# Attention, dense layer and routed experts on one core: value products of two head pairs in one group, transposed weights in the score tile, a later fetch for the first expert

## The chip, the cores and the metric

The kernel runs on one core of a Trainium2 chip. The core has TensorE (PE, with its weight loads as PEld), VectorE (DVE), ScalarE (ACT), GpSimd (POOL), and SyncE (SP), whose queue issues most DMAs here; each works through its instructions in order, and they meet by semaphores. The metric is the device time of one execution in microseconds (us); less is better.

## What is computed

Three steps, each feeding the next, all in fp32 with B, H, S, D = 4, 8, 576, 64:

```python
scores = q @ k.T / 8                         # per batch and head: 576 x 576
kth = 32nd largest of each row               # keep the 32 largest
attn = softmax(where(scores >= kth, scores, -1e9))
x = attn @ v                                 # -> 2304 tokens x 512
h = x @ w_in                                 # 512 x 2048
g = where(h >= 1, h, where(h <= -1, 0, (h + 1)**2 / 4))
x = g @ w_out                                # 2048 x 512
logits = x @ w_gate                          # 8 experts, 288 tokens each,
                                             # filled greedily by largest logit
out[mask_e] = relu(x[mask_e] @ w1[e]) @ w2[e]
```

## The kernel before

The work is recorded as a list of operations with their costs and data dependencies (`Program`), and a planner (`issue`, line 166) gives each engine its order: a list schedule by a rank that the code sets (`P.rank`), refined over ten rounds with the planner's own costs. Operations under `P.group()` stay together on TensorE. There are two such programs, one for each phase; a wait on the chip follows from the data, whatever the planner thought.

First phase (line 365): a loop over 4 batches, 5 blocks of query rows (four of 128, one of 64, j = 4) and 4 pairs of heads. For each pair, `scores` (494) makes two score tiles of 128x576 in a tile of the ring `t_s` (three tiles of two heads each) by way of PSUM bank `pS`; `topk` (541) finds the 32 largest on VectorE, and ScalarE and GpSimd turn the scores into unscaled weights in place. Then `values` (624): TensorE transposes the weights in pieces of 128x128 to `pPT`, ScalarE copies them to `pt`; the last 64 columns of both heads and the reciprocal sums go through `pQ` to `tr`. The products with the values run head by head: c = 0 to 3 are 128 rows deep with 64 columns of values `v` (a 128x64 shape), c = 4 is 64 rows deep (`u`, a 64x64 shape), in two groups. fp32 products take two passes each, so a full pair has 16 passes of the first kind and 4 of the second. VectorE scales the result to `xf`, and ScalarE and GpSimd split it into a high and a low part in `XB` (the dense layer's products are three products of such parts).

The dense layer (`ffn_block`, 687) takes 256 tokens at a time as soon as they are there; its products are planned among the attention's. Block 8, the last, leaves its second product to the second phase. The weights of the dense layer come as 64-bit words and are decoded at the start (`weights`, 444), beside the first pairs.

Second phase (831): `route` (1082) finds one expert's 288 tokens, `places` (1167) their places and indices, `gathers` (1205) fetch the tokens from DRAM with three indirect DMAs from GpSimd, and `expert` (1218) fetches that expert's two matrices with eight DMAs of 512 KB on SP's queue into four buffers `raw`, splits them into high and low parts, and multiplies. For the first expert the gathered tokens meet those of the last dense block in PSUM (`gathered`, 889). The steps of eight experts are planned together.

Of the kernel before, what the change touches and what calls it, by code (L numbers as in the profile page):

```python
# [9 lines left out]
F32 = mybir.dt.float32  # L10
# [37 lines left out]
NF, NM, NSM, NXF, NTR, NQR = 5, 2, 3, 1, 1, 2  # L48
# [230 lines left out]
def kernel(ctx: ExitStack, tc: tile.TileContext, qm, qt, kT, vm, vt,  # L279
# [85 lines left out]
    def first_phase(exact, actx):  # L365
# [78 lines left out]
        def weights(exact):  # L444
            raws = [stage[:, 1024 * i:1024 * i + 1024] for i in range(2)]
            raws += [t.rearrange("p a x -> p (a x)")[:, :1024] for t in (t_s(), t_s(), t_s())[1:]]
            t32s = [stage[:, 2048:2560], spare] + [t_pt().rearrange("p c x -> p (c x)") for _ in range(2)]
# [26 lines left out]
        def load_pair(b, p):  # L474
# [13 lines left out]
            Y.dma_start(out=u_t[:, 0, :], in_=vt[b, :, p])  # L488
            Y.dma_start(out=u_t[:64, 1, :], in_=vt[b, 64:, p])
# [134 lines left out]
        def values(b, j, p, r, s_sb, rinv, wide):  # L624
            P.rank = r + R_PV
            _, v_t, u_t = KV[b, p]
            tail, rb, acc = pQ[:, 0:128], pQ[:, 128:256], pQ[:, 256:384]
            full = j < 4
            w = 128 if full else 64
            pts = []  # L630
            for i in range(2 if full else 1):
                o_ = 64 * i
                with P.group():
                    for c in range(4):
                        T.transpose(pPT[:, 128 * c:128 * c + 128], s_sb[:, i, o_ + 128 * c:o_ + 128 * c + 128], ident)
                pt = t_pt()
                A.activation(pt.rearrange("p c x -> p (c x)"), pPT, AF.Copy)
                pts.append(pt)
            flat = s_sb.rearrange("p a x -> p (a x)")
            tr = t_tr()  # L640
            if full:
                A.activation(wide.rearrange("p (a x) -> p a x", a=2), rinv[:, :2].unsqueeze(2).to_broadcast([128, 2, 64]),
                             AF.Copy)
            with P.group():
                if full:
                    T.transpose(tail, flat[:, 512:640], ident)
                    T.transpose(rb, wide, ident)
                else:
                    T.transpose(tail[:64, :], flat[:, 512:576], ident)
                    T.transpose(rb, rinv[:, 0:1].to_broadcast([128, 128]), ident)  # L650
            if full:
                A.activation(tr.rearrange("p a x -> p (a x)"), pQ[:, :256], AF.Copy)
            else:
                A.activation(tr[:64, 0, :], tail[:64, :], AF.Copy)
                A.activation(tr[:, 1, :], rb, AF.Copy)
            for cs in ((0, 1), (2, 3, 4)):
                with P.group():
                    for c in cs:
                        for h in range(2):
                            hs = slice(64 * h, 64 * h + 64)  # L660
                            if c < 4:
                                rhs = pts[h][:, c, :] if full else pts[0][:, c, hs]
                                T.matmul(acc[hs, :w], v_t[:, c, hs], rhs, start=(c == 0), stop=False)
                            elif full:
                                T.matmul(acc[hs, :w], u_t[hs, 0, :], tr[hs, 0, :], start=False, stop=True)
                            else:
                                T.matmul(acc[hs, :w], u_t[:64, h, :], tr[:64, 0, hs], start=False, stop=True)
            xf = t_xf()
            if full:
                V.tensor_tensor(out=xf, in0=acc, in1=tr[:, 1, :], op=ALU.mult)  # L670
            else:
                for h in range(2):
                    hs = slice(64 * h, 64 * h + 64)
                    V.tensor_tensor(out=xf[hs, :64], in0=acc[hs, :64], in1=tr[hs, 1, hs], op=ALU.mult)
            t0 = b * S + 128 * j
            c0 = 0
            while c0 < w:
                k, off = divmod(t0 + c0, BLK)
                n = min(w - c0, BLK - off)
                if k not in xT:  # L680
                    xT[k] = t_x()
                xh, xl = xT[k][:, 0, p, off:off + n], xT[k][:, 1, p, off:off + n]
                A.activation(xh, xf[:, c0:c0 + n], AF.Copy)
                G.tensor_tensor(out=xl, in0=xf[:, c0:c0 + n], in1=xh, op=ALU.subtract)
                c0 += n
# [80 lines left out]
        def routing_constants():  # L766
            raw = t_pt().rearrange("p c x -> p (c x)")
# [14 lines left out]

        if not exact:
# [21 lines left out]
        t_pt.reset()  # L805
        at, blk = 0.0, 0
# [24 lines left out]
    def second_phase(exact, rctx):  # L831
# [250 lines left out]
        def route(ph):  # L1082
# [331 lines left out]
```

## Time and profile before

| | us |
|---|---|
| median of 3 runs | 1151.74 |
| lowest and highest | 1150.81, 1154.38 |
| the profiled execution's own time | 1145.99 |
| its span, first to last instruction | 1143.7 |
| TensorE busy, share of the span | 1062.0, 93% |
| VectorE busy | 931.2, 81% |
| ScalarE busy | 805.0, 70% |
| GpSimd busy | 697.5, 61% |
| mean granted TensorE clock | 0.963 |

Shares over the whole span mix stages: decoding and the first attention pairs (0 to 120 us), attention and dense layer together (120 to 795), the rest of the dense layer (to 836), routing and the first expert (to 883), and the experts (to the end). TensorE's instructions are pipelined and their ends are modelled, so its busy time includes overlap; differences of starts tell what a group really takes.

### The profile page before, as it was taken

What the parts mean: (1) busy time and instruction counts of PE and PEld (TensorE: products, weight loads), DVE (VectorE), ACT (ScalarE), POOL (GpSimd) and SP (SyncE); (2) the same over time, 40 slices, a digit from 0 to 9 for tenths busy, and PEclk for the clock granted to TensorE, in tenths of its full rate; (3) what the DMA queues carried; (4) which work ended last, traced back from release to release, by engine and by line L of the source; (5) the groups of instructions that cost most, each with busy time, mean ns of one, the idle gap of its engine ahead of it and who ended that gap; (6) DMA issues with size and microseconds to landing.
All of it is one profiled execution on the core that took longest, in us unless ns stands there. A gap on an engine that the chain in (4) does not pass through costs nothing. (4 is left out here: it accounts for less than half of the span.)

```text
span 1143.7 us, 24385 instructions
## 1 busy us (share of the span) xinstructions
PE 1062.0 (93%) x8359; PEld 940.0 (82%) x8359; DVE 931.2 (81%) x2923; ACT 805.0 (70%) x1835; POOL 697.5 (61%) x872
## 2 busy tenths in 40 slices
PE   3677799999999999999999999999997999999995
PEld 2456588888888888898888888888976899999995
DVE  7899999889999999989899999984257997776430
ACT  8899987778888888877888988874313455445541
POOL 6988988977876988757688777763211152223111
PEclk9976599999999999999999999999988999999998
DMA  9744332352212352322134312212315664556500
GB/s 268 220 156 157 111 117 70 109 165 66 92 54 61 96 175 66 92 73 80 61 101 129 93 52 70 82 59 64 117 53 184 208 200 160 169 189 204 175 22 24
DMA packets 62197, 132.81 MB, mean 116 GB/s; under 512 B 15984, under 2 KB 24432, under 8 KB 62064
## 3 DMA queue, kind: packets, MB, share of 16 engines
q1 hardware_dynamic: 58992, 121.73, 33.8%
q0 software_dynamic: 3072, 9.44, 2.5%
q8 instruction: 67, 1.10, 0.4%
q14 instruction: 66, 0.54, 0.2%
HBM read 116.98 MB, written 14.16 MB: 115 GB/s over the span
## 5 line engine op out<-in xcount | busy, mean ns | idle before, releaser
L267 PE MATMUL pH<-XB,W 128*128 128x256 f32 (+1 forms) x2496 | 360.0, 291 | 0.7 <-DVE spare L267 0.3
L267 PEld LDWEIGHTS pH<-XB,W 128*128 128x128 f32 x2496 | 326.5, 189 | 9.7 <-issue 2.9
L267 DVE MAX8 m<-f 128x8 f32<-128x288 f32 x720 | 302.6, 449 | 2.2
L267 POOL TENSOR_TENSOR s<-s,f 128x576 f32<-128x576 f32 x144 | 204.3, 1430 | 30.0 <-ACT f L267 29.1
L267 DVE MATCH_REPLACE8 f<-m,f 128x288 f32<-128x288 f32 x432 | 190.7, 444 | 0.5 <-issue 0.3
L267 PE MATMUL pX<-W,XB 128*128 128x512 f32 x608 | 184.7, 411 | 0.7 <-ACT XB L267 0.7
L267 PE MATMUL pS<-XB 128*128 128x288 f32 (+2 forms) x672 | 145.2, 327 | 31.9 <-POOL XB L267 15.3
L267 POOL TENSOR_TENSOR XB<-stage,XB 128x512 fp32r<-128x512 f32 (+1 forms) x96 | 126.9, 1323 | 59.1 <-ACT XB L267 35.1
L267 PEld LDWEIGHTS pS<-XB 128*128 128x128 f32 x672 | 107.9, 203 | 52.4 <-DVE f L267 18.5
L267 ACT ACTIVATE s<-s,sm 128x576 f32<-128x576 f32 x144 | 111.3, 773 | 22.4 <-POOL s L267 21.3
L267 PEld LDWEIGHTS pX<-W,XB 128*128 128x128 f32 x608 | 107.7, 191 | 19.4 <-issue 2.9
L1210 POOL DMA_INDIRECT xg<-dram_x,idx x24 | 35.4, 1476 | 123.6 <-issue 49.4
L267 ACT ACTIVATE f<-s,t_all 128x576 f32<-128x576 f32 x144 | 108.2, 772 | 2.5
L267 ACT ACTIVATE s<-pS 128x576 f32<-128x576 f32 x144 | 92.7, 643 | 23.2 <-PE pS L267 22.8
L267 PE MATMUL pX<-XB,W 128*128 128x288 f32 x768 | 108.6, 297 | 0.0
L267 DVE TENSOR_TENSOR f<-pS,s 128x288 f32<-128x288 f32 x198 | 86.4, 450 | 22.5 <-ACT s L267 9.2
L267 DVE TENSOR_TENSOR W<-raw,W 128x1024 fp32r<-128x1024 f32 x64 | 76.8, 1218 | 33.5 <-ACT W L267 33.3
L267 PEld LDWEIGHTS pX<-XB,W 128*128 128x128 f32 x768 | 103.5, 188 | 0.0
L267 PE MATMUL pPT<-ident,s 128*128 128x128 f32 x576 | 92.8, 286 | 8.3 <-ACT s L267 6.8
L267 ACT ACTIVATE pt<-pPT 128x512 f32<-128x512 f32 x144 | 84.9, 589 | 17.5 <-PE pPT L267 17.1
L267 PE MATMUL pQ<-pt,v 128*64 128x128 f32 (+1 forms) x1280 | 91.7, 283 | 5.4 <-ACT tr L267 5.2
L1304 POOL DMA_INDIRECT out_dram<-yo,idx x24 | 26.9, 1120 | 109.8 <-ACT yo L267 106.3
(209 smaller groups left out, 1910.2 us busy)
## 6 DMA issues: line engine op xcount, KB each, us to landing
wl<-dram_wlo SPq DMA_DIRECT2D x64, 512.0 KB, 3.4
raw<-in_w_dram SPq DMA_DIRECT2D x64, 512.0 KB, 4.8
qr<-in_qm_dram SPq DMA_DIRECT2D x128, 64.0 KB, 2.4
stage<-in_w_in_dram SPq DMA_DIRECT2D x14, 512.0 KB, 4.2
stage<-in_w_out_dram SPq DMA_DIRECT2D x14, 512.0 KB, 3.3
stage<-in_kT_dram SPq DMA_DIRECT2D x48, 144.0 KB, 2.8
dram_wlo<-wl SPq DMA_DIRECT2D x8, 512.0 KB, 3.1
v<-in_vm_dram SPq DMA_DIRECT2D x16, 256.0 KB, 3.2
```

Source lines behind the costliest of these rows:

```text
L267: P.add(eng, lambda: fn(*args, **kw), cost, reads, writes, lat)
L1210: return nc.gpsimd.indirect_dma_start(out=xg[:, g, :], out_offset=None, in_=x2d[:, :], in_offset=bass.IndirectOffsetOnAxis(ap=idx[:, g:g + ...
L1304: st = nc.gpsimd.indirect_dma_start(out=out, out_offset=bass.IndirectOffsetOnAxis(ap=idx[:, g:g + 1], axis=0), in_=yo, in_offset=None)
```

## The change

- `values` is cut in two. `transposed` makes the transposes of one pair and writes them back over the pair's score tile (its columns 0 to 511, 640 to 1151 and, for the last columns, 512 to 639), so the tiles `pt` and the wide `tr` go; `tr` now holds only the reciprocal sums. Their room goes to a fourth score tile, `s_last`, which also takes the decoded words that `pt` held at the start.
- `values` then runs once for two pairs: 20 products of each pair in one group, to two places of `pQ`, then for both the scaling (into the score tile's first 128 columns, so `xf` goes too) and the split.
- The tail product runs on all 128 rows: each head's 64 rows of `u` stand in their own half, the other half is set to zero once, at the start, and `u` is loaded by two DMAs of 64 rows. For j = 4 the last 64 columns are transposed twice so that they stand in both halves.
- The loads of the next batch's keys and values are recorded after the second pair of a group.
- In `places` the index is written by the reduction itself; `pos` is bounded before instead of the index after.
- For expert 0 the four fetches of the second matrix now wait until the three gathers have landed (they name `xg` as read).

```diff
@@ first_phase @@
+        us = [t_u() for _ in range(4)]
-        t_s = ring(3, tiles=s_tiles)
+        s_last = apool.tile([128, 2, S], F32, name="s3")
+        t_s = ring(4, tiles=s_tiles + [s_last])
-        t_pt = ring(2, [128, 4, 128], F32, "pt")
-        t_tr = ring(NTR, [128, 2, 128], F32, "tr")
-        t_xf = ring(NXF, [128, 128], F32, "xf")
+        t_tr = ring(NTR, [128, 128], F32, "tr")
@@ load_pair @@
-            Y.dma_start(out=u_t[:, 0, :], in_=vt[b, :, p])
-            Y.dma_start(out=u_t[:64, 1, :], in_=vt[b, 64:, p])
+            for h in range(2):
+                Y.dma_start(out=u_t[64 * h:64 * h + 64, h, :], in_=vt[b, 64 * h:64 * h + 64, p])
@@ values @@
+        def transposed(b, j, p, r, s_sb, rinv, wide):
...
+            def last():
+                with P.group():
+                    if full:
+                        T.transpose(tail, flat[:, 512:640], ident)
+                        T.transpose(rb, wide, ident)
+                    else:
+                        T.transpose(tail, flat[:, 448:576], ident)
+                        T.transpose(tail[:64, :], flat[:, 512:576], ident)
+                        T.transpose(rb, rinv[:, 0:1].to_broadcast([128, 128]), ident)
+                A.activation(flat[:, 512:640], tail, AF.Copy)
+                A.activation(tr, rb, AF.Copy)
+            if not full:
+                last()
+            pts = []
+            for i in range(2 if full else 1):
+                pt = flat[:, 640 * i:640 * i + 512]
+                with P.group():
+                    for c in range(4):
+                        T.transpose(pPT[:, 128 * c:128 * c + 128], pt[:, 128 * c:128 * c + 128], ident)
+                A.activation(pt, pPT, AF.Copy)
...
+        def values(b, j, ps, r, made):
...
+            accs = [pQ[:, 256 + 128 * n:384 + 128 * n] for n in range(2)]
             with P.group():
...
-                                T.matmul(acc[hs, :w], u_t[:64, h, :], tr[:64, 0, hs], start=False, stop=True)
+                                T.matmul(acc[hs, :w], u_t[:, h, :], flat[:, 512:640] if full else flat[:, 512:640][:, hs],
+                                         start=False, stop=True)
...
+                xf = flat[:, :128]
...
+        P.rank = -10.0
+        for u_t in us:
+            G.memset(u_t[64:, 0, :], 0.0)
+            G.memset(u_t[:64, 1, :], 0.0)
...
-                    values(b, j, p, at, s_sb, rinv, wide)
+                    made.append(transposed(b, j, p, at, s_sb, rinv, wide))
+                    if p % 2:
+                        values(b, j, (p - 1, p), at, made)
+                        made = []
                     at += 1.0 if j < 4 else 0.6
-                    if j == 4 and b + 1 < B:
-                        P.rank = at + R_K
-                        load_pair(b + 1, p)
+                    if j == 4 and b + 1 < B and p % 2:
+                        for x in (p - 1, p):
+                            P.rank = at + R_K
+                            load_pair(b + 1, x)
@@ route, places @@
+            most = rt([128, NT], F32, "most")
+            V.tensor_scalar(most, tk, 2.0 * N * E, None, op0=ALU.mult)
...
-            V.scalar_tensor_tensor(out=pos, in0=sc, scalar=pS[:, 1, 8:9], in1=tk, op0=ALU.add, op1=ALU.mult)
+            V.scalar_tensor_tensor(out=pos, in0=sc, scalar=pS[:, 1, 8:9], in1=most, op0=ALU.add, op1=ALU.min)
...
-            tok = rt([96, 3], F32, "tok")
-            V.tensor_reduce(out=tok, in_=pS[:96, 1, :6].rearrange("p (a g) -> p g a", a=2), axis=AX, op=ALU.add)
-            V.tensor_scalar(idx, tok, N - 1.0, None, op0=ALU.min)
+            V.tensor_reduce(out=idx, in_=pS[:96, 1, :6].rearrange("p (a g) -> p g a", a=2), axis=AX, op=ALU.add)
@@ expert @@
-                P.add("sync", partial(fetch, raw, i // 4, i % 4), 1450, [ei[0:1, 0:1]], [raw], 2500)
+                P.add("sync", partial(fetch, raw, i // 4, i % 4), 1450, [ei[0:1, 0:1]] + [xg] * (early and i > 3), [raw], 2500)
```

## Rows read from the trace of the kernel before

**Rows 1.** Busy us by stage (PE, PEld, DVE, ACT, POOL), granted clock, DMA share, GB/s

```profile
60.00:120.00 60.00, 44.67 (x264) 36.00 (x263) 58.85 (x177) 58.14 (x152) 50.56 (x63) 0.67 0.47 152
120.00:240.00 120.00, 112.58 (x848) 95.95 (x848) 108.64 (x347) 100.36 (x249) 105.77 (x135) 0.91 0.35 109
240.00:480.00 240.00, 235.96 (x1889) 204.90 (x1889) 228.95 (x789) 203.51 (x481) 188.31 (x247) 1.00 0.29 90
480.00:600.00 120.00, 119.89 (x959) 105.73 (x957) 105.49 (x342) 94.90 (x220) 85.88 (x108) 1.00 0.27 84
600.00:720.00 120.00, 118.50 (x943) 101.77 (x942) 116.10 (x404) 103.76 (x246) 97.27 (x128) 1.00 0.28 87
790.00:830.00 40.00, 40.00 (x320) 37.96 (x319) 13.01 (x31) 13.55 (x23) 9.66 (x10) 1.00 0.31 109
874.00:878.00 4.00, 3.88 (x29) 3.48 (x30) 1.30 (x2) 2.02 (x2) 0.00 (x0) 0.50 0.38 144
```

**Rows 2.** TensorE in order of time, an unsplit pair: start, us, operation, count

```profile
279.03 1.09 PE L267 MATMUL pQ<-pt,v 128*64 128x128 f32 x16
280.06 0.44 PE L267 MATMUL pQ<-tr,u 64*64 64x128 f32 x4
280.42 1.33 PE L267 MATMUL pH<-XB,W 128*128 128x256 f32 x9
```

**Rows 3.** TensorE in order of time, a split pair's first half

```profile
261.27 0.66 PE L267 MATMUL pQ<-pt,v 128*64 128x128 f32 x8
261.86 0.80 PE L267 MATMUL pS<-XB 128*128 128x288 f32 x4
```

**Rows 4.** Waits of weight loads, 120 to 795: us in total, times, longest

```profile
PEld pQ L267 <- issue: 18.7, 96, 0.4
```

**Rows 5.** One pair's score tile in order of time, 242 to 280, three engines

```profile
242.34 0.65 ACT L267 ACTIVATE s<-pS 128x576 f32<-128x576 f32 x1
...
256.40 0.24 DVE L267 MAX8 m<-m 128x8 f32<-128x16 f32 x2
...
269.38 0.60 ACT L267 ACTIVATE pt<-pPT 128x512 f32<-128x512 f32 x1
...
273.51 0.63 ACT L267 ACTIVATE s<-pS 128x576 f32<-128x576 f32 x1
...
274.55 0.28 DVE L267 TENSOR_TENSOR xf<-pQ,tr 128x128 f32<-128x128 f32 x1
...
279.14 0.47 POOL L267 TENSOR_TENSOR XB<-xf,XB 128x128 fp32r<-128x128 f32 x1
```

**Rows 6.** SP, GpSimd and TensorE in order of time, first expert

```profile
862.44 5.81 SPq L1233 DMA_DIRECT2D raw<-in_w_dram  x4
...
865.43 1.77 POOL L1210 DMA_INDIRECT xg<-dram_x,idx  x1 [0.30 <-issue]
...
867.90 0.46 PE L267 MATMUL pH<-ident,xg 96*128 96x96 f32 x2 [1.00 <-DMA xg<-dram_x,idx]
...
874.12 0.74 PE L267 MATMUL pH<-ident,xg 96*128 96x96 f32 x2 [3.03 <-DMA xg<-dram_x,idx]
...
895.54 1.36 PE L267 MATMUL pX<-XB,W 128*128 128x288 f32 x9
```

**Rows 7.** Groups of instructions: shape, count, busy us, mean ns, idle before

```profile
L267 PEld LDWEIGHTS pQ<-pt,v 128*64 128x64 f32 x1280 | 68.0, 144 | 26.7 <-issue 9.9 <-ACT tr L267 7.8 <-ACT XB L267 2.6
...
L267 ACT ACTIVATE tr<-pQ 128x256 f32<-128x256 f32 x64 | 24.1, 377 | 1.7 <-PE pQ L267 1.7
...
L267 DVE TENSOR_SCALAR idx<-tok 96x3 int32<-96x3 f32 x8 | 1.4, 180 | 0.0
```

**Rows 8.** TensorE in order of time, end of the first phase

```profile
793.40 0.45 PE L267 MATMUL pQ<-pt,v 128*64 128x64 f32 x8
...
805.47 0.40 PE L267 MATMUL pX<-W,XB 128*128 128x512 f32 x1
```

**Rows 9.** All 24 gathers of the tile xg, last line

```profile
DMA to landing us min/median/max: 3.4/5.9/11.9
```

More of the change, by code (lines that the diff above doesn't have):

```diff
@@ L445, in weights @@
             raws = [stage[:, 1024 * i:1024 * i + 1024] for i in range(2)]
-            raws += [t.rearrange("p a x -> p (a x)")[:, :1024] for t in (t_s(), t_s(), t_s())[1:]]
-            t32s = [stage[:, 2048:2560], spare] + [t_pt().rearrange("p c x -> p (c x)") for _ in range(2)]
+            raws += [t.rearrange("p a x -> p (a x)")[:, :1024] for t in s_tiles[1:3]]
+            t32s = [stage[:, 2048:2560], spare] + [s_last.rearrange("p a x -> p (a x)")[:, a:a + 512] for a in (0, 512)]
             for n in range(32):
@@ L622, in first_phase @@
         xT, late = {}, []
-        def values(b, j, p, r, s_sb, rinv, wide):
+        def transposed(b, j, p, r, s_sb, rinv, wide):
             P.rank = r + R_PV
-            _, v_t, u_t = KV[b, p]
-            tail, rb, acc = pQ[:, 0:128], pQ[:, 128:256], pQ[:, 256:384]
+            tail, rb = pQ[:, 0:128], pQ[:, 128:256]
             full = j < 4
[L629 to L638, printed above, removed]
             flat = s_sb.rearrange("p a x -> p (a x)")
@@ L643, in values @@
                              AF.Copy)
-            with P.group():
[L645 to L658, printed above, removed]
+            def last():
[18 more added lines that the diff above has]
+                A.activation(pt, pPT, AF.Copy)
+                pts.append(pt.rearrange("p (c x) -> p c x", c=4))
+            if full:
+                last()
+            return pts, flat, tr
+        def values(b, j, ps, r, made):
+            P.rank = r + R_PV
+            full = j < 4
+            w = 128 if full else 64
+            accs = [pQ[:, 256 + 128 * n:384 + 128 * n] for n in range(2)]
+            with P.group():
+                for p, (pts, flat, tr), acc in zip(ps, made, accs):
+                    _, v_t, u_t = KV[b, p]
+                    for c in range(5):
                         for h in range(2):
@@ L663, in values @@
                                 T.matmul(acc[hs, :w], v_t[:, c, hs], rhs, start=(c == 0), stop=False)
-                            elif full:
-                                T.matmul(acc[hs, :w], u_t[hs, 0, :], tr[hs, 0, :], start=False, stop=True)
-                            else:
-                                T.matmul(acc[hs, :w], u_t[:64, h, :], tr[:64, 0, hs], start=False, stop=True)
[L668 to L674, printed above, removed]
@@ L675, in values @@
-            t0 = b * S + 128 * j
[L676 to L685, printed above, removed]
+                            else:
+                                T.matmul(acc[hs, :w], u_t[:, h, :], flat[:, 512:640] if full else flat[:, 512:640][:, hs],
+                                         start=False, stop=True)
@@ new lines, in values @@
+            t0 = b * S + 128 * j
+            for p, (pts, flat, tr), acc in zip(ps, made, accs):
+                xf = flat[:, :128]
+                if full:
+                    V.tensor_tensor(out=xf, in0=acc, in1=tr, op=ALU.mult)
+                else:
+                    for h in range(2):
+                        hs = slice(64 * h, 64 * h + 64)
+                        V.tensor_tensor(out=xf[hs, :64], in0=acc[hs, :64], in1=tr[hs, hs], op=ALU.mult)
+                c0 = 0
+                while c0 < w:
+                    k, off = divmod(t0 + c0, BLK)
+                    n = min(w - c0, BLK - off)
+                    if k not in xT:
+                        xT[k] = t_x()
+                    xh, xl = xT[k][:, 0, p, off:off + n], xT[k][:, 1, p, off:off + n]
+                    A.activation(xh, xf[:, c0:c0 + n], AF.Copy)
+                    G.tensor_tensor(out=xl, in0=xf[:, c0:c0 + n], in1=xh, op=ALU.subtract)
+                    c0 += n
@@ L804, in first_phase @@
         t_s.reset()
-        t_pt.reset()
-        at, blk = 0.0, 0
+        at, blk, made = 0.0, 0, []
         for b in range(B):
```

4 lines of the change are left out of this document (2 added, 2 removed).

## The prediction

> **What bounds the kernel now.** I read the busy time by stage first [rows 1]. From 240 to 720 us TensorE is busy 99% of the time, and from 790 to 830 all of it; VectorE comes close behind, 95.4% from 240 to 480, 96.8% from 600 to 720, but only 90.5% and 87.9% in the two stages around. So TensorE sets the pace of the first phase, with VectorE a few per cent behind. Before 120 VectorE is at 98.1% with a slow TensorE; nothing that shortens TensorE's work counts there.
>
> Then TensorE's own order of time, for what its busy time hides [rows 2, 3]. Starts count here, since the modelled ends overlap. Sixteen passes of a pair's products with the values take 1.03 us from their start to the next group's (279.03 to 280.06), eight take 0.59 (261.27 to 261.86). One more pass thus costs 0.055 us, and 16 of them leave 0.15 us over. The four passes with the tail tile, on 64 rows, take 0.36 us, of which 0.22 are passes and 0.14 are left over. The same loss shows as weight loads that wait for nothing visible: 18.7 us in 96 waits, 0.195 us each [rows 4]. I read it as the price of each change of shape in the array (128x128 to 128x64, to 64x64, and back).
>
> Third, the life of one score tile [rows 5], and last the way from routing into the first expert [rows 6], where TensorE waits for three gathers, 1.00 us before the first lands and 3.03 before the last, with two transposes of 0.46 us all it does between 867.9 and 874.1; from 874 to 878 its granted clock is then 0.50 [rows 1], the lower of its two levels, 1.2 GHz.
>
> **Products on 128 rows, two pairs as one group.** Counting runs in TensorE's order of time from 120 to 795 us: 74 pairs, 93 runs of products on 128 rows (19 pairs are split in two by other work), 74 runs on 64 rows, the last product at 793.40 [rows 8]. That is 93 changes in, 74 to the smaller shape, 74 out of it and 19 out after a first half: 260. One group for two pairs has two, so 74 for 37 groups. 186 fewer at 0.15 us are 28 us (26 at 0.14, 36 at 0.195). The number of passes stays, and a pass is as long on 128 rows as on 64 (0.055 us both). Before 120 I count nothing.
>
> The Trainium skill (TensorE: Matmul & The Clock Gate, Part 3, What overlaps and what doesn't) says that a weight load overlaps a running matmul only where the row groups differ; the 64-row tails lie in two row groups and the new 128-row tails don't, so by that rule the change would lay bare loads that are hidden now. The trace disagrees, as the next sentence shows.
>
> A load of a 128x64 tile is 0.144 us long [rows 7], yet a further pass on 128 rows costs 0.055 in all, load included: the loads are hidden on 128 rows too. I add nothing. If they were not, 80 pairs with four loads of 0.144 would cost 46 us.
>
> Can the stage use 28 us? Let VectorE reach the 98.1% of its densest stage. From 240 to 480 its 228.95 us then need 233.4, which frees 6.6 us where TensorE offers 28 x 240/675 = 9.9; from 600 to 720 1.7 where 5.0 are offered; from 120 to 240 and from 480 to 600 VectorE has 9 and 12 us of room, so the offered 5.0 each; 3.1 after 720. Sum 21.4 while attention runs. The other 6.6 can come back after it: block 7 of the dense layer runs on TensorE until 805.5, 12 us past the last product of attention [rows 8]; TensorE is busy all of 790 to 830 [rows 1].
>
> **Transposed weights over the weights.** Score tiles go from a ring of three to one of four. Today a tile is free once its transposes are done; afterwards it holds the transposed weights and then the scaled product until ScalarE and GpSimd have split that, and the first tile of a group waits for its partner too. [rows 5] follow one such second pair: scores copied at 242.34, top-k done at 256.64, last transposed copy 269.98, scaled product 274.83, GpSimd's subtraction 279.61. The scores three pairs on start at 273.51, so pairs come every 10.4 us. With the change the even pair that took its scores at 273.51 could do so only after 279.6. VectorE has the two pairs between to work on, 20.8 us; the loop from the end of the second pair's top-k to the next pair's is 23.0 us to the subtraction plus some 2.2 us for scores and fold, 25.2. But 4.3 us of it are GpSimd doing other work first (274.83 to 279.14), which nobody hurries today because only the dense layer waits; taken away, it is 20.9 against 20.8. So the loop lies just at its limit: the bounds of this part are 0 (the order adapts) and all 21.4 us of the attention's gain, or more. I take half, 11 us kept, since the one pair followed sits at the limit rather than on a side.
>
> Small costs: 16 more tail transposes on TensorE; at 0.144 us, the length of a weight load [rows 7], 2.3 us, and hardly less, as a transpose needs its load: 2. ScalarE copies tail and reciprocals in two instructions instead of one of 0.377 us, at most 64 x 0.377 = 24 us more of its work [rows 7]; it is busy 79 to 86%, off the path: 0, or up to 3 if the loop binds. Eight memsets on GpSimd at the start have no row; the nearest is its subtraction over 128 columns, 0.47 us [rows 5], so 0 to 4 us, ahead of a stage in which VectorE is full: 0 on the path. The last two pairs' products now end together, 1 us. The next batch's loads, with ScalarE's copy and GpSimd's subtraction for the keys, are recorded a pair later, behind the second pair's work on all three queues: hidden by the two pairs of score work that the planner keeps in flight, and if that cover were gone, one half pair's time per batch, some 5 us, three times. Phase one: 11 + 6.6 - 2 - 1 = 14.6 us less, at best 25.
>
> **Expert 0's second matrix held back.** The four fetches go out between 862.4 and 868.3, together with three gathers; the third gather, issued at 865.43, lets TensorE go at 874.12, 8.7 us later [rows 6]. Without that traffic I take 4 us from issue to landing (the shortest of the 24 is 3.4 [rows 9]), so 869.4: 4.7 us sooner. If TensorE's clock then doesn't fall, the 4 us at half clock from 874 save up to 2 more. Against it: the fetches now wait on SP's queue, and behind them stand two stores of the last token block and the next expert's number and fetches. The stores are needed by the next expert's gathers only, a round of routing later. The matrix itself is fetched up to 7 us later than now; its last fetch goes out at 868.3 and the first product with it starts at 895.5, so 27 us of cover shrink to 20. If that cover were gone, each us late would be a us lost. I take 5.5 us, bounds 0 and 7.5; a loss would need more than that cover.
>
> The Trainium skill (DMA: Bandwidth & Descriptors, Queues, rings and completion order) says that each DMA engine takes turns between the queues it has work for. By that the gathers would have half the engines already and the hold would be worth the lower bound, 5.5 us less than I take.
>
> What speaks against that bound is the row: the third gather is 96 rows of 512 fp32 numbers, 0.2 MB, and each fetch beside it 0.5 MB; at half share it would not have taken longer than all four fetches took to be issued (5.81 us).
>
> **Routing.** One small instruction of VectorE (0.18 us [rows 7]) leaves the way to each index and one of the like joins off it. With eight experts that is 1.4 us if every index is waited for and 0 if none is; later experts' tokens are fetched while TensorE still works, so I take the first two: 0.4 us.
>
> **Sum.** 14.6 + 5.5 + 0.4 = 20.5, about 21 us less than the profiled execution's own 1145.99: 1125. The median of the runs is 1151.74, 1.005 times that, so 1130.5.
>
> **The rivals.** *The loop doesn't bind* (the planner hurries the split): 25 + 5.5 + 0.4 = 31 less, 1115, as a median 1121, and 1112 with the dearer change of shape and the better gather. For it: today the next scores start 3.5 us after the release (269.98 to 273.51 [rows 5]), so there is something to give. Against: VectorE's 96%, which leaves little to absorb a late score.
>
> *The loop eats the gain*: attention ends when it does now, only 6.6 - 3 + 5.9 remain, 1142; with 4 us lost again 1146.
>
> *The loop makes it slower*: the place is the score tile's release, the price every microsecond past 20.8 us per group, over the 24 full groups outside the first batch. At 1.3 us over, 31 us are lost and 10 gained, 1167, 1173 as a median; kept exactly as in [rows 5], four times that loss. It decides from 20.8 us on.
>
> *The loads lie bare* (the rule on row groups): 46 us, 1176.
>
> *The hold does nothing*: 5.5 us less gain, 1136, within the forecast's own range of 1124 to 1141.
>
> **How the numbers follow.** Forecast 0.50; loop doesn't bind 0.17; gain eaten, 1141 to 1155, 0.17, of which 0.10 lies below 1148.3 and 0.07 within; slower 0.15; bare loads 0.01. A measurement of this kernel tells about 0.3%, 3.5 us, from no change. Faster 0.77, same 0.07, slower 0.16. The range from 1113 to 1152 leaves out the slow cases and a sliver below.
>
> **What would show it.** Right: no 64x64 products left, 40 runs of 40 passes, issue waits before them near a third; VectorE over 96% from 240 to 720; the last scaled product some 10 us sooner; the gathers' waits of 6.3 us down to about 2. Wrong: TensorE waiting for scores or for transposes with VectorE idle, or GpSimd's subtractions named as what releases a score group; or the experts' matrix waited for at the second layer.

## The result: slower, by 0.7%

The changed kernel takes 1161.15 us (median of 4 runs, 1160.05 to 1162.45) where the kernel before takes 1151.28 beside it: 1.0070 times as long by the estimate over all runs of both, 95% interval 1.0043 to 1.0098 (the two medians alone give 1.0086). 1130.5 was predicted, 1113 to 1152 as the range, and slower had a chance of 0.16. The profiled execution's own time is 1161.94, its span 1160.1; that of before was a quick one (1145.99), so stretches of the two profiles differ by some 16 us where the medians differ by 10.

The stages of the changed kernel, columns as in [rows 1]:

```profile
60.00:120.00 60.00, 42.42 (x258) 36.27 (x260) 56.20 (x167) 55.92 (x150) 46.02 (x57) 0.68 0.46 146
120.00:240.00 120.00, 106.44 (x780) 94.30 (x777) 100.01 (x322) 99.17 (x247) 101.14 (x128) 0.86 0.32 102
240.00:480.00 240.00, 228.11 (x1902) 204.01 (x1901) 221.69 (x768) 199.34 (x490) 183.05 (x240) 0.99 0.30 91
480.00:600.00 120.00, 118.73 (x940) 107.18 (x940) 109.44 (x371) 99.45 (x240) 91.69 (x116) 1.00 0.26 82
600.00:720.00 120.00, 113.99 (x926) 99.38 (x923) 110.46 (x384) 99.89 (x247) 93.57 (x123) 1.00 0.27 86
```

TensorE fell from 98% to 95% of the time between 240 and 480, and VectorE did not rise into the room: 92.4%, after 95.4%. No engine is full any more there, nor from 600 to 720; only from 480 to 600 is TensorE still at 99%. From 120 to 240 VectorE lost 8.6 us of work done, TensorE 6.1. This is what a loop between engines looks like: each waits for another, in turn.

TensorE in order of time shows that its own saving came as meant; two pairs are one run of 40 passes:

```profile
781.87 1.09 PE L267 MATMUL pQ<-s,v 128*64 128x128 f32 x16
782.79 0.39 PE L267 MATMUL pQ<-s,u 128*64 128x128 f32 x4
783.01 1.04 PE L267 MATMUL pQ<-s,v 128*64 128x128 f32 x16
783.88 0.39 PE L267 MATMUL pQ<-s,u 128*64 128x128 f32 x4
784.20 1.20 PE L267 MATMUL pX<-W,XB 128*128 128x512 f32 x4
```

By starts, 2.33 us for two pairs, where one unsplit pair took 1.39 [rows 2]; both are also the medians of all such runs after 120 us (37 and 55). All 40 groups are whole. The waits of 120 to 795 us (in total, times, longest), changed kernel first, then two rows of the kernel before:

```profile
PEld pS L267 <- DVE f L267: 22.9, 33, 2.3
...
PE pS L267 <- DVE f L267: 19.7, 30, 1.9
...
DVE f L267 <- ACT s L267: 15.1, 21, 2.3
...
DVE sm L267 <- ACT sm L267: 9.6, 8, 2.4
...
PEld pQ L267 <- issue: 5.0, 17, 0.4
...
ACT s L267 <- POOL XB L267: 3.8, 6, 1.0
```

```profile
PEld pS L267 <- DVE f L267: 7.7, 17, 1.4
...
PE pS L267 <- DVE f L267: 5.3, 11, 1.0
```

The loads' waits with no visible cause went from 18.7 us in 96 [rows 4] to 5.0 in 17, and in their place TensorE, wanting to make scores, waits for VectorE to read the scores before (5.3 us to 19.7), and VectorE for ScalarE's scores (9.2 us to 15.1). The row that names the score tile's release, ScalarE's copy of scores waiting for GpSimd, has 3.8 us only. Probably it hides because the planner knows that the tile is not free and puts the copy later; so the release has to be looked for in the order of time. Engine by engine (GpSimd, ScalarE, VectorE):

```profile
302.82 0.46 POOL L267 TENSOR_TENSOR XB<-s,XB 128x128 fp32r<-128x128 f32 x1
...
305.88 0.47 POOL L267 TENSOR_TENSOR XB<-s,XB 128x128 fp32r<-128x128 f32 x1
...
321.94 0.61 POOL L267 TENSOR_TENSOR XB<-s,XB 128x64 fp32r<-128x64 f32 x2
```

```profile
303.68 0.63 ACT L267 ACTIVATE s<-pS 128x576 f32<-128x576 f32 x1
...
306.08 0.65 ACT L267 ACTIVATE s<-pS 128x576 f32<-128x576 f32 x1 [0.17 <-PE pS L267]
...
311.15 0.64 ACT L267 ACTIVATE s<-pS 128x576 f32<-128x576 f32 x1
...
314.92 0.64 ACT L267 ACTIVATE s<-pS 128x576 f32<-128x576 f32 x1
...
322.65 0.64 ACT L267 ACTIVATE s<-pS 128x576 f32<-128x576 f32 x1
```

```profile
300.80 0.27 DVE L267 TENSOR_TENSOR s<-pQ,tr 128x128 f32<-128x128 f32 x1
...
302.21 0.27 DVE L267 TENSOR_TENSOR s<-pQ,tr 128x128 f32<-128x128 f32 x1
```

GpSimd's subtraction for an even pair ends at 303.28, and the scores of the pair four later go into that tile at 303.68; it ends at 322.55, and the next go in at 322.65. Worked out alike for 18 even pairs of batches 1 to 3 (the first three blocks of rows), the tile is written again 0.39 us (median) after its release, 15 of 18 times within 1 us; in the kernel before it was 3.1 us after the last transposed copy, never within 1. In [rows 5] that gap was 3.5. In the first batch it is the same: 9 of 10 even pairs' tiles are written again within 1 us. The hold is long because the first pair waits for the second: from first scores to scaled product an even pair takes 35.4 us (median of the 24 full even pairs of batches 1 to 3), 29.9 before; odd pairs stay at 29.8 (29.5). The odd pair's first scores follow 7.5 us behind (311.15), the next even pair's 11.5 us after those: pairs run two by two.

In the second phase the first expert's gathers (GpSimd), what TensorE had left to wait for, ScalarE's splits after them, and SP's queue:

```profile
876.60 1.54 POOL L1230 DMA_INDIRECT xg<-dram_x,idx  x1 [22.36 <-DVE I L267]
878.45 0.92 POOL L1230 DMA_INDIRECT xg<-dram_x,idx  x1 [0.31 <-issue]
879.68 1.61 POOL L1230 DMA_INDIRECT xg<-dram_x,idx  x1 [0.30 <-issue]
```

```profile
883.49 0.46 PE L267 MATMUL pH<-ident,xg 96*128 96x96 f32 x2 [1.41 <-DMA xg<-dram_x,idx]
...
896.22 0.19 PE L267 MATMUL pS<-SC,s 128*128 128x1 bf16 x1 [3.95 <-DVE SC L267]
896.57 1.81 PE L267 MATMUL pH<-XB,W 128*128 128x288 f32 x6 [0.16 <-DVE XB L267]
```

```profile
888.10 1.06 ACT L267 ACTIVATE W<-raw 128x1024 fp32r<-128x1024 f32 x1 [5.81 <-DMA raw<-in_w_dram]
889.66 1.06 ACT L267 ACTIVATE W<-raw 128x1024 fp32r<-128x1024 f32 x1 [0.51 <-DMA raw<-in_w_dram]
892.49 1.06 ACT L267 ACTIVATE W<-raw 128x1024 fp32r<-128x1024 f32 x1 [1.76 <-DMA raw<-in_w_dram]
```

```profile
883.60 0.33 SPq L267 DMA_DIRECT2D dram_x<-yo  x1
884.20 1.64 SPq L1253 DMA_DIRECT2D raw<-in_w_dram  x3
```

The third gather lets TensorE go 3.8 us after its issue (8.7 before [rows 6]). One point is to be put right: naming `xg` as read in the fetch makes no wait of its own on the chip; it moves the fetches behind the gathers in the planner's order, and on SP's queue they then stand (884.20) behind a store of tokens (883.60) that waits for the gathers.

### The profile page after: what moved, and what is told of

Read it like the earlier page. It is cut to its first block, busy times and chain, and to the rows that moved or that the text cites. A ratio compares the mean times of both kernels' runs of the same rounds, so it can differ in the third digit from the quotient of the medians.

```text
span 1160.1 us, 24540 instructions
## 1 busy us (share of the span) xinstructions
PE 1051.9 (91%) x8375; PEld 954.2 (82%) x8375; DVE 924.8 (80%) x2923; ACT 809.9 (70%) x1899; POOL 701.4 (60%) x880
## 3 DMA queue, kind: packets, MB, share of 16 engines
q1 hardware_dynamic: 57968, 121.47, 32.8%
## 4 chain that ended last, share of the span: by engine, by line
PE 52%; DVE 21%; ACT 10%; POOL 8%; issue 4%; DMA 3%; another core or an unknown queue 0%; SPq 0%; DVEq 0%; POOLq 0%; ACTq 0%
PE pH L267 21%; PE pX L267 19%; DVE f L267 8%; DVE m L267 7%; PE pS L267 6%; ACT s L267 5%; PE pQ L267 4%; POOL s L267 3%; PE pPT L267 3%; POOL XB L267 2%; POOL f L267 2%; DVE stage L267 2%; ACT f L267 1%; ACT stage L267 1%; DMA raw<-in_w_dram 1%
## 5 line engine op out<-in xcount | busy, mean ns | idle before, releaser
L267 PE MATMUL pH<-XB,W 128*128 128x256 f32 (+1 forms) x2496 | 370.1, 295 | 3.7 <-ACT XB L267 0.8
L267 PEld LDWEIGHTS pH<-XB,W 128*128 128x128 f32 x2496 | 335.5, 193 | 13.4 <-issue 3.9
L267 PE MATMUL pS<-XB 128*128 128x288 f32 (+2 forms) x672 | 149.0, 332 | 41.7 <-DVE f L267 28.7
L267 POOL TENSOR_TENSOR XB<-stage,XB 128x512 fp32r<-128x512 f32 (+1 forms) x96 | 127.4, 1327 | 72.4 <-ACT XB L267 49.8
L1230 POOL DMA_INDIRECT xg<-dram_x,idx x24 | 38.1, 1586 | 121.1 <-DVE idx L267 70.2
L267 ACT ACTIVATE XB<-pH 128x288 fp32r<-128x288 f32 x94 | 37.2, 409 | 82.7 <-PE pH L267 65.8
L267 ACT ACTIVATE s<-pPT 128x512 f32<-128x512 f32 x144 | 85.2, 592 | 13.1 <-PE pPT L267 12.8
```

The costliest lines, as they stand in the source:

```text
L267: P.add(eng, lambda: fn(*args, **kw), cost, reads, writes, lat)
L1230: return nc.gpsimd.indirect_dma_start(out=xg[:, g, :], out_offset=None, in_=x2d[:, :], in_offset=bass.IndirectOffsetOnAxis(ap=idx[:, g:g + ...
```

## Experiments

All runs at a glance. Ratio: to the kernel before on the same chip, with its 95% interval. Runs lie on several chips, so medians of two rows can differ by some us more or less than their ratios say: against the changed kernel, E3, E5 and E6 gain 23.7, 18.7 and 12.2 us by medians, some 20, 17 and 10 by ratios. The last four columns are stretches of each profile in us: start of the span to the last scaled product of the first batch; the other three batches; from there to the routing's first product on TensorE; from there to the end.

| | median | ratio | batch 0 | batches 1-3 | to routing | rest |
|---|---|---|---|---|---|---|
| before | 1151.28 | 1 | 254.1 | 540.7 | 44.1 | 304.8 |
| changed | 1161.15 | 1.0070 (1.0043-1.0098) | 262.6 | 546.3 | 46.6 | 304.6 |
| E1 | 1141.62 | 0.9927 (0.9902-0.9952) | 253.8 | 535.9 | 44.0 | 305.0 |
| E2 | 1165.94 | 1.0133 (1.0109-1.0157) | 266.3 | 551.5 | 46.6 | 302.0 |
| E3 | 1137.42 | 0.9895 (0.9871-0.9919) | 251.8 | 537.2 | 45.7 | 301.6 |
| E4 | 1161.00 | 1.0091 (1.0069-1.0114) | 264.4 | 543.4 | 46.6 | 306.5 |
| E5 | 1142.46 | 0.9925 (0.9903-0.9948) | 253.0 | 536.0 | 46.0 | 306.0 |
| E6 | 1148.96 | 0.9985 (0.9972-0.9999) | 267.7 | 529.6 | 45.7 | 303.6 |
| E7 | 1162.34 | 1.0097 (1.0073-1.0121) | 255.0 | 553.7 | 46.6 | 305.8 |
| E8 | 1147.07 | 0.9969 (0.9951-0.9987) | 251.6 | 539.8 | 44.6 | 306.1 |
| E9 | 1139.21 | 0.9896 (0.9870-0.9922) | 251.9 | 537.4 | 45.7 | 303.0 |
| E10 | 1348.26 | 1.1695 (1.1658-1.1732) | 302.3 | 715.9 | 33.1 | 298.3 |
| E11 | 1327.90 | 1.1522 (1.1485-1.1560) | 292.0 | 697.6 | 34.9 | 301.3 |
| E12 | 1328.58 | 1.1539 (1.1505-1.1573) | 297.2 | 697.6 | 34.2 | 297.5 |
| E13 | 1163.95 | 1.0101 (1.0077-1.0126) | 261.1 | 549.1 | 47.3 | 305.4 |
| E14 | 1170.99 | 1.0165 (1.0137-1.0192) | 286.0 | 531.9 | 46.6 | 303.9 |
| E15 | 1149.11 | 0.9975 (0.9958-0.9992) | 252.3 | 540.4 | 46.4 | 306.5 |
| E16 | 1173.82 | 1.0185 (1.0157-1.0214) | 281.9 | 543.2 | 45.8 | 305.5 |
| E17 | 1133.10 | 0.9861 (0.9841-0.9880) | 252.7 | 529.2 | 45.6 | 302.0 |
| E18 | 1150.95 | 1.0012 (0.9998-1.0027) | 256.2 | 542.7 | 46.7 | 302.7 |

The theory to start with: TensorE's saving is real, and the loop through the score tiles eats it and more. Rivals: TensorE's time is not on the path at all; the planner's new order is an unlucky one; the hold loses what it gains. TensorE's granted clock explains nothing here: the profile of the changed kernel has 0.955 and that of before 0.963, but E7 is as slow as the changed kernel at 0.964.

**E1 and E2: the saving alone, and taken out again.** In both the planner is given the old operands, so that every engine keeps its order. E1 is the kernel before with the tail product on 128 rows (shown in short; the clearing of `u` and the 16 more transposes that it needs are in it):

```diff
-  T.matmul(acc[hs, :w], u_t[hs, 0, :], tr[hs, 0, :], start=False, stop=True)
+  T.matmul(acc[hs, :w], u_t[:, h, :], tr[:, 0, :], start=False, stop=True)
```

E2 is the changed kernel with it back on 64:

```diff
-  T.matmul(acc[hs, :w], u_t[:, h, :], flat[:, 512:640] if full else flat[:, 512:640][:, hs],
+  T.matmul(acc[hs, :w], u_t[hs, h, :], flat[hs, 512:640] if full else flat[hs, 512:640][:, hs],
            start=False, stop=True)
```

> The kernel before, with only the last product of each pair of heads on all 128 rows: the spare halves of the u buffers are cleared once and the values' last 64 rows go to the two halves; nothing is grouped by two pairs, no buffer is shared, the copies still go into their own tiles, and every engine keeps its order instruction by instruction (the last query tile of a batch gets one more 128-row transpose per pair, 16 in all, under 3 us). About 100 shape changes of TensorE go away. Loop theory (the gain is there, and the release of the score tiles in the new kernel eats it): faster than before by 8 to 20 us, 1131 to 1143 on the chip where before takes 1151. Rival 1 (TensorE's time is not on the path of the attention): within 3 us of before. Rival 2 (the new order that the planner found by chance is what costs): says nothing on the sign here, since the order is the old one.

> The changed kernel with the last products back on 64 rows each, in the same order on every engine: three shape changes more in each group of two pairs, some 120 in all at about 0.15 us, so 18 us more of TensorE. Loop theory: the loop through the score tile holds the products as a link, so each group pays its 0.5 us in series: 8 to 18 us above the changed kernel, 1169 to 1179. Rival 1 (TensorE not on the path): within 3 us of the changed kernel.

Loads' waits from 120 to 795 us, E1 and then E2:

```profile
PEld pQ L267 <- issue: 9.1, 40, 0.4
```

```profile
PEld pQ L267 <- issue: 20.5, 104, 0.4
```

In E1 the waits halve (18.7 to 9.1) and 8.0 us are gained (1141.62 against 1149.64 on that chip), at the lower edge of what was expected: TensorE's time is on the path of the kernel before, and the first rival falls. In E2 the waits rise by 15.5 us and the time by some 5 (1165.94 against 1161.15; by the ratios 1.0133 and 1.0070, 0.6%): less than the 8 to 18 expected. By these figures two thirds of such a cost fall, in the changed kernel, into time in which TensorE waits anyway.

**E3, E5, E6: pairing and held tile.** E5 forms a values group for each pair:

```diff
-                    if p % 2:
-                        values(b, j, (p - 1, p), at, made)
-                        made = []
+                    values(b, j, (p,), at, made)
+                    made = []
```

E6 gives the scaled product a tile of its own, so that the score tile is free when the products have read it; E3 has both edits.

```diff
+        t_xf = ring(1, [128, 128], F32, "xf")
...
-                xf = flat[:, :128]
+                xf = t_xf()
```

> The changed kernel with the values of each pair as a group of their own as soon as its weights are transposed, and with a tile of its own for the scaled product (one buffer, as before the change), so that a score tile comes free when the products have read it and not after GpSimd's subtraction; transposed weights still overwrite the weights, last products on 128 rows. Loop theory: the even pair no longer waits for the odd one and the lockstep of two pairs is gone; the gain comes out, 1133 to 1146 (15 to 28 us below the changed kernel). Rival 1: 1150 to 1155. Rival 2 (planner): anywhere between.

> The changed kernel with one edit: the values of each pair as a group of their own; the scaled product still overwrites the head of the score tile, so the tile is still held until GpSimd's subtraction. Loop theory, with the pairing as the culprit (in the trace of the changed kernel the even pair's product comes 5 to 8 us later after its scores than before, the odd one's does not): most of the gain of the kernel with both edits comes out, 1137 to 1144. If the held tile (the subtraction) is the culprit: 1152 to 1160. Planner theory: anywhere.

> The changed kernel with the other edit alone: a tile of its own for the scaled product (one buffer), values still by two pairs. The two products of a group then share one buffer, so the second waits for GpSimd's subtraction of the first. Pairing as the culprit: 1155 to 1163, near the changed kernel. Held tile as the culprit: 1138 to 1148.

Unpairing takes 18.7 us off, the own tile 12.2, both 23.7. E3 is faster than the kernel before. The table tells them apart by place: E6 is the quicker kernel in batches 1 to 3 (529.6) and the slowest of these in batch 0 (267.7). So both suspects are guilty, and neither expectation for E6, pairing or tile alone, is met. Both act on one loop: in E5, where the tile is held as before but each pair goes by itself, it is written again 4.1 us after its release (the same 18 even pairs), once within 1 us.

**E7, E8: another order of the same work**, in the changed kernel and in the kernel before, by the rank of the transposes and values (the fifth number, `R_PV`):

```diff
-R_QL, R_QS, R_QK, R_MK, R_PV, R_K, R_F, R_U = -4.0, -2.0, -1.2, 0.5, 1.0, 1.0, 1.5, 0.9
+R_QL, R_QS, R_QK, R_MK, R_PV, R_K, R_F, R_U = -4.0, -2.0, -1.2, 0.5, 1.1, 1.0, 1.5, 0.9
```

> The changed kernel with the rank at which the planner takes the transposes and the values raised from 1.0 to 1.1 (in units of one pair's scores): same instructions, another order on every engine. It measures what an arbitrary new order of the same work is worth. Loop theory: within 5 us of the changed kernel, 1156 to 1166. Planner theory: the changed kernel's order is an unlucky one, and this one comes out 8 us or more away from it.

> The kernel before with the same shift of that rank: the same measure for the old structure. Loop theory: within 5 us of the kernel before. Planner theory: 8 us or more away, and above it, if the old order was a lucky one.

The new order moves the changed kernel by +0.3% and the kernel before by -0.3%, 4 us at most; the 10 to 28 us between kernels here are not likely to be chance of the order (two other orders are all that was run), though less than 4 us may be. In E7 the loss sits elsewhere (batch 0 ends at 255.0, the others take 553.7) with the same sum, 808.7 against 808.9: the order shifts the loss and doesn't remove it. It also means that up to 8 us of a difference by place, batch 0 against the others, can be the order's.

**E4, E9: without the hold**, E4 made from the changed kernel, E9 from E3:

```diff
-  ... [ei[0:1, 0:1]] + [xg] * (early and i > 3), [raw], 2500)
+  ... [ei[0:1, 0:1]], [raw], 2500)
```

> The changed kernel without the hold of expert 0's second matrix. If the hold is worth what was predicted: 3 to 6 us slower than the changed kernel. If what it gains at the gathers is given back in ScalarE's and VectorE's queues by the end of expert 1, as the trace has it (+3.3 us at expert 0, -0.1 at expert 1): within 1.5 us of the changed kernel.

> The fastest kernel so far (values per pair, a tile of its own for the scaled product, 1137.4) without the hold of expert 0's second matrix. In its trace the hold brings expert 0 forward by 2 us against the kernel before and expert 7 by 3.3 us, and the 3.2 us gap of VectorE in expert 1 that the changed kernel has is not there. If the hold has a worth that the gap in expert 1 hides in the changed kernel: 2 to 5 us slower, 1139.5 to 1142.5. If the hold is worth nothing anywhere: within 1.5 us of 1137.4.

Nothing that can be measured either way (1161.00 against 1161.15; ratios 0.9896 for E9 and 0.9895 for E3; each ratio's interval is some 3 us either way). In the profiles the rest is 1.9 and 1.4 us shorter with the hold.

**E10 to E12: a fifth score tile, with room taken from the tiles `f`.** E10 has the first edit, E11 also a fifth tile `s4` in `t_s`, E12 also the own tile of E6.

```diff
-NF, NM, NSM, NTR, NQR = 5, 2, 3, 2, 2
+NF, NM, NSM, NTR, NQR = 3, 2, 3, 2, 2
```

> A control for the next two: the changed kernel with 3 instead of 5 of the tiles into which VectorE writes the first pass over the scores (this frees the room for one more score tile). No theory has a number for it: 1161 to 1190, as that ring becomes a loop of its own.

> The control with a fifth score tile. Loop theory (two score tiles are freed late and at once): 6 us or more faster than the control. If the pairing costs by something else than the tiles (products of two pairs in one uninterrupted run of TensorE, the late scaled product itself): within 3 us of the control.

> The control with a fifth score tile and a tile of its own for the scaled product. Loop theory: both reliefs together, 12 us or more faster than the control. Otherwise near the control with the own tile alone, which took 12 us off the changed kernel: then the fifth tile adds nothing.

1348.26, 1327.90 and 1328.58 us: three tiles `f` bind by themselves, 187 us. The control is far outside the 1161 to 1190 expected. The fifth tile gives 20 us there and the own tile nothing more, but under another bound; this says little on the changed kernel.

**E13 to E16: the fifth tile with room taken elsewhere** (one buffer for raw keys, decode buffers inside the fifth tile). E13 and E14 are paired, E15 and E16 unpaired; E13 and E15 don't use the tile for scores.

```diff
+        s_more = apool.tile([128, 2, S], F32, name="s4")
...
-        t_s = ring(4, tiles=s_tiles + [s_last])
+        t_s = ring(5, tiles=s_tiles + [s_last, s_more])
...
-        t_kr = ring(2, tiles=[stage[:, 1536 + S * i:1536 + S * i + S] for i in range(2)])
+        t_kr = ring(1, tiles=[stage[:, 1536:1536 + S]])
```

> Control: the changed kernel with one buffer instead of two for the raw keys of the next batch and two decode buffers moved into a fifth score-sized tile that the scores don't use. 1158 to 1172 (the changed kernel has 1161), the part above 1161 being the price of the single key buffer.

> The control with the fifth tile in the ring of the scores; values still by two pairs, scaled product still in the tile. Loop theory: the next group's first scores no longer wait for the two tiles that come free together, 8 to 20 us faster than the control, 1140 to 1155. If pairing costs by itself (two pairs' products and scaled products late whatever the tiles): within 3 us of the control.

> The same control for the kernel with values per pair (1142 with two key buffers): 1140 to 1150.

> Values per pair with the fifth tile. Loop theory: four tiles are nearly enough when each comes free by itself, so the fifth is worth less than in the paired kernel: 0 to 6 us faster than its control. If it is worth as much as in the paired kernel, the pairing is not what makes the tiles scarce.

Both are slower with the tile, by 7 and 25 us, against every expectation. The table shows where: batch 0 ends 24.9 and 29.6 us later. The tile holds the decode's words there, until the last weights are decoded, and the ring makes scores wait for it: the fifth pair's first scores come at 133.4 us in E14, at 72.4 in E13. In batches 1 to 3, where nothing else uses it, the tile gives the paired kernel 17.2 us (549.1 to 531.9) and costs the unpaired one 2.8. That is what the loop theory says of those batches; but it is read from one profile each, so it was put to a test of its own.

**E17, E18: pairing from the second batch on**, with the scaled product's own tile (E17) and without (E18):

```diff
-                    if p % 2:
+                    if not b:
+                        values(b, j, (p,), at, made)
+                        made = []
+                    elif p % 2:
```

> Values per pair in the first batch, by two pairs in the other three, and a tile of its own for the scaled product. If the pairing costs only in the first batch and the held tile only after it: the first batch as in the unpaired kernel (last scaled product near 252), the other three as in the paired one with the own tile (529.6 us instead of 537.2): 7 us under the fastest so far, 1128 to 1133. If the pairing costs everywhere: 1138 to 1150.

> The same without the own tile: the scaled product overwrites the score tile and holds it until GpSimd's subtraction. Two causes in two places: first batch near 253, the other three as in the changed kernel (546.3 us), so 10 to 17 us above the kernel with the own tile, 1142 to 1152. If the loss of the changed kernel is all of the first batch's: within 4 us of the kernel with the own tile.

E17 is 1133.10, the fastest of all, 1.4% under the kernel before; E18 1150.95. Both are where two causes put them, E17 to within 0.1 us of its range; E18's first batch ends 3 us later than expected and its others are 4 us shorter. Busy us from 60 to 250 and 250 to 790, columns as in [rows 1], of before, changed kernel, E17 and E18:

```profile
60.00:250.00 190.00, 166.31 (x1185) 140.01 (x1184) 177.35 (x556) 166.19 (x419) 164.50 (x207) 0.84 0.40 127
250.00:790.00 540.00, 535.04 (x4270) 464.42 (x4269) 495.72 (x1688) 445.92 (x1050) 407.34 (x534) 1.00 0.27 83
```

```profile
60.00:250.00 190.00, 158.00 (x1137) 139.10 (x1137) 163.80 (x514) 162.52 (x414) 156.76 (x195) 0.81 0.37 119
250.00:790.00 540.00, 519.42 (x4199) 463.36 (x4200) 492.22 (x1692) 445.03 (x1094) 405.66 (x531) 0.99 0.27 83
```

```profile
60.00:250.00 190.00, 168.92 (x1219) 146.27 (x1219) 180.11 (x569) 170.40 (x439) 164.89 (x206) 0.82 0.41 127
250.00:790.00 540.00, 526.57 (x4343) 473.92 (x4340) 494.00 (x1691) 447.12 (x1096) 409.50 (x535) 1.00 0.27 83
```

```profile
60.00:250.00 190.00, 163.92 (x1190) 142.43 (x1191) 175.32 (x558) 169.11 (x435) 164.14 (x205) 0.83 0.41 126
250.00:790.00 540.00, 518.00 (x4219) 460.27 (x4219) 493.06 (x1683) 445.35 (x1088) 405.81 (x531) 1.00 0.26 82
```

In the first batch VectorE is the full engine, 93% before and 95% in E17; the paired products starve it (86%). After it, TensorE is idle 20.6 us in the changed kernel and 22.0 in E18, where the tile is held, against 13.4 in E17, which gets through more instructions in that time (4343 against 4199 and 4219 matmuls). Its next scores no longer wait for the split; ScalarE and VectorE of E17 in order of time:

```profile
304.32 0.63 ACT L267 ACTIVATE s<-pS 128x576 f32<-128x576 f32 x1
...
319.94 0.63 ACT L267 ACTIVATE s<-pS 128x576 f32<-128x576 f32 x1
```

```profile
304.89 0.27 DVE L267 TENSOR_TENSOR xf<-pQ,tr 128x128 f32<-128x128 f32 x1
...
306.69 0.27 DVE L267 TENSOR_TENSOR xf<-pQ,tr 128x128 f32<-128x128 f32 x1
```

The scores at 304.32 start ahead of the group's scaled product (304.89), not after its subtraction. Between E17 and E18 no line of code differs but that tile's (with it the planner's order): 17.9 us, 1.5%, of which 13.5 lie in batches 1 to 3. In E18 the reuse is back at 0.39 us after the release, 15 of 18 times within 1 us.

## Why the prediction was wrong, step by step

*What bounds the kernel.* Right: TensorE's time is on the path (E1). After the change no engine's busy time is the bound from 240 to 480 and from 600 to 720.

*The price of a change of shape.* Mis-sized. 260 changes were counted and each priced at 0.15 us, three of them for an unsplit pair. But [rows 2] leave over only 0.29 us for such a pair (0.15 and 0.14), and [rows 4] hold 18.7 us in all, less than the 28 that were to be saved. The changed kernel has 2.33 us for two pairs, 1.165 each instead of 1.39: 0.225 us saved a pair, for 74 pairs 16.7, and some 3 for the 19 pairs that were split: about 20, not 28. That the stage can use most of what TensorE saves fits: batches 1 to 3 of E17 are 11.5 us shorter than before, where 60 pairs at 0.225 make 13.5 (one profile each, and E17 has other buffers too).

The rule in the Trainium skill on loads in the same row group (TensorE: Matmul & The Clock Gate, Part 3, What overlaps and what doesn't) would have laid the loads bare; 40 passes on the same 128 rows in 2.33 us, 0.058 each, show that it doesn't hold here.

*The loop.* This is the step that failed. Place and mechanism were named (the tile held until ScalarE and GpSimd have split the product, the partner waited for), and the estimate of 20.9 us against 20.8 put it at its limit; then half of the attention's gain, 10.7 us, was taken off, on the ground that one pair followed sits at the limit. The runs put it at 28 (1161.15 against 1133.10): 17.9 for the held tile once the first batch is unpaired, the rest, 10.2, for pairing in the first batch. The rival had it at 1.3 us over the limit per group and 31 us lost; the 13.5 us of the held tile in batches 1 to 3, over 24 full groups, are 0.56 a group (and the whole delay of [rows 5] kept, 4.4 us over, would have been 3.4 times the rival's loss, not four). Two terms of the estimate were too kind. The 4.3 us of other work on GpSimd were "taken away", since the planner could hurry the subtraction, which left 0.5 us from scaled product to its end; it did hurry it, but only to 2.1 us (median of the 24 full even pairs, 3.2 before; for odd pairs it stayed at 3.2), 1.6 more than the estimate had. And the 20.8 us for two pairs came from the one pair followed: in batches 1 to 3 of the kernel before, scores of full pairs came every 9.2, 10.6 and 9.1 us, so two pairs took 18.2 to 21.3. With the first correction the loop lies over its limit everywhere, with the second in two of the three batches, and half the gain was too much to keep.

*The first batch.* "Before 120 I count nothing" and the rival's count "outside the first batch" left out where 10 to 16 us were lost (E18 against the changed kernel, 10.2; E17 against E6, 15.9; of the 10.2, the profiles have 6.4 in that batch). VectorE at 98.1% in [rows 1] said that less TensorE work buys nothing there; it should also have said that late scores cost there. The own tile didn't help in that batch (E6 267.7); the reuse of the tile within 1 us, 9 times of 10, says that it is the same loop there, with the partner waited for. In E6 the tile comes free with the group's last product, and 4 of 10 even pairs' tiles are still written again within 1 us of that; but its two scaled products also share one buffer. What each of these costs in that batch was not separated.

*The hold.* Its gathers came as predicted: 3.8 us instead of 8.7 (4 was taken), TensorE's waits down to 1.41, and the stretch after them is at full clock where [rows 1] have 0.50:

```profile
884.00:888.00 4.00, 4.00 (x48) 3.59 (x48) 2.23 (x6) 0.00 (x0) 0.00 (x0) 1.00 0.77 242
```

But the cover was looked for at the wrong place. The prediction asked when TensorE first needs the matrix (20 us left); ScalarE splits it, in order, ahead of the token split and the next routing, so ScalarE waits 5.81 us at 888.10, VectorE behind it, and TensorE 3.95 at 896.22. The first layer starts 41.0 us after the routing instead of 44.4, yet the whole rest is 304.6 instead of 304.8: of 5.5 us, E4 and E9 leave nothing that can be measured, 1.4 to 1.9 by the profiles. As the prediction read the rule in the Trainium skill on queues taking turns (DMA: Bandwidth & Descriptors, Queues, rings and completion order), the hold was worth 0. That is the worth measured, but not by that way: without the fetches beside them the gathers did land 4.9 us sooner.

*The sum.* About 8 us less saved on TensorE, 17 more lost to the loop and 5.5 not gained by the hold turn the 20.5 forecast into some 10 lost; 9.9 were measured (roughly, since the runs lie on several chips).

*Small costs and routing.* The two copies of ScalarE, the memsets and the routing's 0.4 us can't be told apart in these runs; E3 has the two copies and is 1% faster than the kernel before all the same.

*What would show it.* Of the signs of right came the runs of 40 passes, the waits at a third (27%) and the gathers; VectorE's 96% and the earlier last scaled product (it came 14.1 us later) did not. Of the signs of wrong came TensorE held up at the scores with VectorE idle. The subtraction as the named releaser came in 3.8 us of waits only, and in the order of time in full.

## What to carry to other kernels

Before two results are joined into one group, or a result is written over its source, follow the buffer from its first write to its last reader on whichever engine that is, and compare the loop with the period of the other engines in every stage; take the periods and delays from many rounds, not from one. Here a loop estimated at its limit was over it. In a planned order such a loop hardly shows as a wait on the buffer (3.8 us here); it shows as a reuse within a fraction of a us of the release, time after time. And a held transfer has its cover at the first engine that touches it in order, not at the one that needs it last.

## What was not expected of the hardware

In the changed kernel VectorE stands still for 3.16 us in expert 1, in front of an instruction whose TensorE product was done; the order of time, and one of the three DMA queues at work from 938 to 939 us (packets, MB, share of 16 engines):

```profile
941.01 0.17 DVE L267 TENSOR_SCALAR ge<-pQ 128x8 bf16<-128x8 f32 x1 [3.16 <-remote]
```

```profile
q8 instruction: 1, 0.02, 6.4%
```

One transfer of instructions lands in that gap. E5 to E7 and E13 to E16 show the same gap; E2, E3, E10 to E12, E17 and E18 don't, though E2 has the same order and such a transfer at the same point, and none of the kernels without the hold does (before, E1, E4, E8, E9). What decides is open. Where the gap is, the copies of expert 1's results start 34.6 us after those of expert 0 (35 in E5 and E6), without it 30.8 to 32.8: the difference is about the 3.3 us that the hold had gained at the first layer. It is not the reason for the hold's small worth, since E3 has no gap and gains no more.
